# The reciprocal row sums of an attention and soft-MoE kernel: multiplied onto the transposed product through a DMA round trip, with k's factor moved into the maximum's pass and the dispatch logits summed in PSUM

## The chip, the cores and the metric

One core of a Trainium2 chip runs the whole program. The time is the device time of one execution in microseconds (us); three executions of the kernel before gave 566.71, 567.28 and 567.25, median 567.25. Everything is float32, except the last product with the combine weights, which runs in a rounded float32 format.

## The reference, cut to what matters

```python
# attention: 8 batches x 8 heads, 576 tokens, head size 64
scores = q @ k.T / 8
thresh = max(scores, -1) - tau
attn   = exp(where(scores >= thresh, scores, -1e9) - max(scores, -1))
attn   = attn / (sum(attn, -1) + 1e-9)
x      = attn @ v                       # then heads are put side by side: x is 4608 x 512
# soft MoE: 8 experts, 4 slots each (32 slots), phi 512 x 32
logits = x @ phi
d = exp(logits - logits.max(0));  d /= d.sum(0) + 1e-9     # dispatch weights, over all tokens
slot_input = d.T @ x                                       # 32 x 512
slot_out[e] = relu(slot_input[e] @ w1[e]) @ w2[e]          # per expert, 512 -> 1024 -> 512
c = exp(logits - logits.max(1));  c /= c.sum(1) + 1e-9     # combine weights, per token
out = c @ slot_out
```

Two facts matter below. The row sum of the attention weights belongs to a query, so 1 / row sum may be multiplied onto the weights or, later, onto the product with v. And the logits are linear in x.

## The kernel before, in words

**Stages.** The 64 (batch, head) problems are done as 32 pairs of heads, pair p = 4 b + j; after each fourth pair `dispatch(b)` works on the batch. Partitions 0 to 63 hold the first head of the pair, 64 to 127 the second. After the last pair a tail computes the experts (`stage1`, `stage2`) and the combination. The tail's weights w1 and w2 are 64 tiles of 512 KB: 26 are loaded beside the attention (two a pair, from the fourth pair on), the others as SBUF comes free near its end.

**One pair.** 576 queries of two heads are nine tiles i of 128 rows (two heads' last 64 queries share the ninth, `pL`). For each tile: TensorE writes the scores to PSUM (L517, L522). VectorE makes one pass over them (L531), which writes the negated scores to SBUF (`ss`) and their row minimum (`nmx`). GpSimd adds tau to it (`thr`, L547). ScalarE takes the exponential (`p`, L544). VectorE masks by the threshold and sums the row (`r`, L551). TensorE transposes the masked tiles (`ptr`, L441), ScalarE copies them to SBUF (`pTa`, `pTb`, `pTl`), and TensorE multiplies by v (L621, two pieces of 256 and 320 queries). That gives `xT`: 128 rows (two heads' 64 features) by 576 queries. It is transposed once more into `x` (tokens by features).

**Where the row sums and the factor of k go, before.** k is multiplied by 1/8 (`flag8`, 0 where tau is negative) in SBUF by GpSimd before its first use (L497; for the first pair by VectorE, in halves). The reciprocals are made in two pieces: for the ninth tile (L558, L561), which GpSimd then scales itself (`pL`, L565), and for the other eight (L569, L572), which GpSimd multiplies onto `x`, where a query is a partition (L636). As `xT` needs the same factor for the logits, `x` is then transposed back by TensorE (L641) and copied over `xT` by ScalarE (L644). The last pair (`late`) scales its weights instead.

**Dispatch, before.** The four pairs' products with phi stand in four row groups of one PSUM bank (L700), ScalarE copies all 576 columns to SBUF (`l4`), TensorE transposes them (L712), and VectorE adds the four parts (L717, L719). The result is transposed again to get the slots' maximum (L732), the maximum is brought back over the partitions, subtracted (L744, L748) and exponentiated (`d`, `dl`). The tokens 512 to 575 of two batches share tiles, so odd batches do more. `weigh` sums the dispatch weights and the weighted tokens into `csum` and `acc`.

**What sets the order.** Every instruction of the attention is recorded with an engine, an assumed duration, a due time and the buffers it uses. `Order.plan` plays them through: on each engine the ready instruction with the smallest due time is taken, if the buffers it needs are free (`SLOTS` says how many there are; score tiles and other PSUM uses share four regions of two banks). `TABLE` overrides due times one by one. The result is a fixed order on each engine. So an instruction that waits holds up all that stands behind it on its engine, and SyncE's DMAs are issued in the recorded order too.

Of the kernel before, what the change touches and what calls it, by code (L numbers as in the profile page):

```python
# [10 lines left out]
F32 = mybir.dt.float32  # L11
F32R = mybir.dt.float32r
AF = mybir.ActivationFunctionType
# [9 lines left out]
    k=2, q=2, vv=2, r=3, ri=3, nmx=4, thr=4, p2=4, pL=1, pTa=1, pTb=1, pTl=1, l4=1,  # L23
    ss=4, xT=5, x=1, xl=1, ll=1, d=1, M=2, f=2, dl=1,
# [6 lines left out]
AWAY = tuple(range(9))  # L31
# [3 lines left out]
WARM = 38  # L35
FILL = 14
NHOST = 20
TABLE = {}
for _n, _v in (
    ("first", [  # L40
        -69.29, -40.08, -54.39, -166.86, 33.12, -19.81, -19.80, -168.20, -0.40, -236.51, -236.95, -153.88, 373.52, -143.51,
        -213.06, -159.92, -239.98, 369.22, -217.49, None, None, None, None, -253.40, -126.63, -318.67, -88.12, -177.39,
        278.76, -134.26, -253.19, -236.64, -230.43, 370.37, -209.27, None, None, None, None, -339.56, -230.28, -296.07,
        -250.71, 93.46, -214.46, -219.12, 327.41, -239.17, 115.81, -98.67, -235.60, 351.28, -15.35, None, None, None,
        None, 112.02, -216.81, 98.22, -232.40, -233.77, 362.06, -234.27, -288.73, -106.13, -268.80, 322.40, -178.31, 363.65,
        -236.80, None, None, 118.41, -219.40, -224.78, -93.89, -126.64, 366.17, -247.36, 346.23, -178.30, 337.45, -316.13,
        -131.26, -162.52, -225.24, -157.75, 100.52, -243.70, 140.26, -257.76, -282.45, -236.24,
    ]),
    ("pair", [
        371.05, 316.17, 334.99, -1401.66, 316.16, 123.84, 29.03, 245.92, -1430.28, -54.33, 123.33, -50.94, 281.90, -1430.27,  # L50
        -51.83, None, None, None, None, 127.29, 267.41, 123.83, -11.83, 236.94, -1401.65, 331.60, 124.87, 111.68,
        324.56, -1392.66, -17.22, None, None, None, None, 127.78, 273.77, 125.61, 320.90, 124.88, -55.71, 264.20,
        -1401.66, 3.52, 128.01, -29.96, 282.13, -1402.51, -69.32, None, None, None, None, 127.15, 305.89, 128.38,
        -19.31, 318.29, -1392.84, 362.75, 127.50, -39.14, 365.12, -1401.65, -20.82, -1422.29, 119.74, None, None, 135.78,
# [25 lines left out]
    ("soft", [  # L80
        215.59, 346.40, -349.85, 338.95, 233.69, 238.87,
    ]),
    ("new", [
        921.26, -1421.98, 51.86,
    ]),
):
# [1022 lines left out]
```

## Time and profile before

| | us |
|---|---|
| profiled execution, whole | 567.02 |
| its span, first to last instruction | 565.2 |
| PE busy | 536.4 (95%) |
| DVE busy | 476.1 (84%) |
| ACT busy | 458.2 (81%) |
| POOL busy | 257.9 (46%) |
| attention and dispatch, to the last score tiles' end | about 0 to 489 |
| tail | about 489 to 565 |

PE is TensorE, DVE VectorE, ACT ScalarE, POOL GpSimd; SPq is SyncE's queue, which issues all DMAs. A busy PE is not PE at its peak, since matmuls are pipelined and their ends modelled. A row of the timeline gives the start, the duration, the engine, the line and operation, the tiles written and read, how many instructions were merged, and in square brackets the idle time before it with what ended it. A row of the groups gives busy time and mean ns of one after the first bar, idle time before them after the second. A row of the windows gives, for one stretch, the busy time of PE, PEld (weight loads), DVE, ACT and POOL with instruction counts, then the granted clock, the share of the DMA engines in use and GB/s. The mean granted clock of the execution was 0.985.

### The profile page before, as it was taken

What the parts mean: (1) busy time and instruction counts of PE and PEld (TensorE: products, weight loads), DVE (VectorE), ACT (ScalarE), POOL (GpSimd) and SP (SyncE); (2) the same over time, 40 slices, a digit from 0 to 9 for tenths busy, and PEclk for the clock granted to TensorE, in tenths of its full rate; (3) what the DMA queues carried; (4) which work ended last, traced back from release to release, by engine and by line L of the source; (5) the groups of instructions that cost most, each with busy time, mean ns of one, the idle gap of its engine ahead of it and who ended that gap; (6) DMA issues with size and microseconds to landing.
All of it is one profiled execution on the core that took longest, in us unless ns stands there. A gap on an engine that the chain in (4) does not pass through costs nothing. (4 is left out here: it accounts for less than half of the span.)

```text
span 565.2 us, 17532 instructions
## 1 busy us (share of the span) xinstructions
PE 536.4 (95%) x6652; PEld 341.4 (60%) x6652; DVE 476.1 (84%) x1342; ACT 458.2 (81%) x784; POOL 257.9 (46%) x489
## 2 busy tenths in 40 slices
PE   8799999999999999999999999999999998899990
PEld 7566665666566666666666656666666565544470
DVE  5899998999999999998999899999999899322192
ACT  3699998999889999999899989998999889411171
POOL 1555553455345544554455545555555347311030
PEclk9799999999999999999999999999999999999996
DMA  7355555465446544432333333333333312899488
GB/s 170 70 160 164 163 161 154 121 188 177 102 127 178 167 132 140 102 94 52 81 88 89 88 89 87 88 89 87 89 87 88 88 63 54 319 404 409 194 357 313
DMA packets 31988, 82.99 MB, mean 147 GB/s; under 512 B 4640, under 2 KB 12832, under 8 KB 31904
## 3 DMA queue, kind: packets, MB, share of 16 engines
q1 hardware_dynamic: 31904, 81.87, 48.3%
q8 instruction: 53, 0.87, 0.7%
q14 instruction: 31, 0.25, 0.1%
HBM read 72.42 MB, written 9.44 MB: 145 GB/s over the span
## 5 line engine op out<-in xcount | busy, mean ns | idle before, releaser
L531 DVE TENSOR_SCALAR_CACHE_REDUCE ss<-ps 128x576 f32<-128x576 f32 x288 | 209.2, 749 | 23.4 <-ACT l L446 8.1
L547 POOL TENSOR_SCALAR thr<-nmx,pabs 128x1 f32<-128x1 f32 x288 | 130.0, 453 | 177.7 <-DVE ss L531 165.8
L551 DVE SCALAR_TENSOR_TENSOR p<-ss,thr,p 128x576 f32<-128x576 f32 x256 | 205.2, 823 | 3.8 <-POOL thr L547 2.7
L544 ACT ACTIVATE p<-ss,nmx 128x576 f32<-128x576 f32 x256 | 190.4, 781 | 13.0 <-DVE ss L531 13.0
L517 PE MATMUL ps<-k,q 64*128 64x288 f32 x1024 | 165.6, 430 | 3.9 <-POOL k L497 1.8
L441 PEld LDWEIGHTS ps<-ident,p 64*128 64x128 f32 x2304 | 92.9, 140 | 29.5 <-DVE p L551 7.0
L441 PE MATMUL ps<-ident,p 64*128 64x64 f32 x2304 | 105.2, 226 | 3.9 <-DVE ss L531 1.9
L517 PEld LDWEIGHTS ps<-k,q 64*128 64x128 f32 x1024 | 84.9, 190 | 36.1 <-ACT pTb L446 8.8
L446 ACT COPY pTb<-ps 128x1024 f32<-128x1024 f32 (+1 forms) x95 | 83.7, 881 | 2.6 <-PE ps L441 1.4
L621 PE MATMUL ps<-pTb,vv 128*64 128x320 f32 x512 | 76.0, 439 | 2.1 <-ACT pTa L446 1.8
L446 ACT COPY pTa<-ps 128x1024 f32<-128x1024 f32 x64 | 65.7, 1026 | 2.3 <-PE ps L441 2.1
L621 PE MATMUL ps<-pTa,vv 128*64 128x256 f32 x512 | 62.3, 385 | 1.5 <-DVE ss L531 0.8
L621 PEld LDWEIGHTS ps<-pTb,vv 128*64 128x64 f32 x512 | 34.1, 136 | 31.6 <-ACT pTa L446 3.1
L621 PEld LDWEIGHTS ps<-pTa,vv 128*64 128x64 f32 x512 | 33.9, 136 | 27.7 <-DVE ss L531 11.8
L621 PE MATMUL ps<-pTl,vv 128*64 128x256 f32 (+1 forms) x256 | 41.9, 406 | 0.0
L446 ACT COPY xT<-ps 128x256 f32<-128x256 f32 (+1 forms) x63 | 25.2, 400 | 13.5 <-PE ps L621 13.5
L446 ACT COPY pTl<-ps 128x256 f32<-128x256 f32 x64 | 23.8, 372 | 13.1 <-PE ps L441 12.3
L636 POOL TENSOR_TENSOR x<-x,ri 128x512 f32<-128x512 f32 x31 | 33.1, 1069 | 1.6 <-ACT x L446 1.5
L558 POOL TENSOR_SCALAR ri<-r 128x1 f32<-128x1 f32 (+1 forms) x36 | 20.0, 555 | 23.2 <-DVE pL L551 21.4
L565 POOL TENSOR_SCALAR pL<-pL,ri 128x576 f32<-128x576 f32 x32 | 26.5, 830 | 8.4 <-DVE ri L561 5.7
L899 POOL TENSOR_TENSOR c<-lall,crow 128x512 f32<-128x512 f32 x9 | 9.3, 1043 | 39.9 <-PE ct L433 39.9
L497 POOL TENSOR_SCALAR k<-k,flag 128x576 f32<-128x576 f32 x31 | 23.8, 769 | 7.0 <-DMA k<-in_kT 6.4
(134 smaller groups left out, 564.8 us busy)
## 6 DMA issues: line engine op xcount, KB each, us to landing
w<-in_w SPq DMA_DIRECT2D x44, 512.0 KB, 6.6
q<-in_qT SPq DMA_DIRECT2D x62, 288.0 KB, 4.3
vv<-in_vt SPq DMA_DIRECT2D x32, 320.0 KB, 4.0
host<-in_w SPq DMA_DIRECT2D x20, 512.0 KB, 6.4
k<-in_kT SPq DMA_DIRECT2D x62, 144.0 KB, 4.5
out<-w SPq DMA_DIRECT2D x8, 512.0 KB, 3.3
out<-host SPq DMA_DIRECT2D x8, 512.0 KB, 6.1
out<-host SPq DMA_DIRECT2D x4, 256.0 KB, 4.7
```

Source lines behind the costliest of these rows:

```text
L441: nc.tensor.transpose(out=s[:, g, c:c + 64], in_=ins[g], identity=ident[rows[g], rows[g]], tile_position=(64 * g, 0))
L446: G.add("ACT", 51 + 0.833 * n, nom, lambda: nc.scalar.copy(*io()), r, w)
L497: sc = lambda e, kc=kc: lambda: e.tensor_scalar(out=kt.t[:, kc], in0=kt.t[:, kc], scalar1=flag8, **one)
L517: nc.tensor.matmul(s.t[:, g, 0:HS], qt.t[rows[g], h, c * 128:(c + 1) * 128], kt.t[rows[g], h * HS:(h + 1) * HS], start=True, stop=True, ti ...
L531: dve(674, t + OFF['mx'], [s], [ss, nmx], lambda s=s, ss=ss, nmx=nmx: nc.vector.tensor_scalar(out=ss.t.rearrange("p (a k) -> p a k", a=2), ...
L544: G.add("ACT", 668 if away else 630, t + OFF['ex'], lambda sv=sv, nmx=nmx, view=view, away=away: nc.scalar.activation(view().rearrange("p ...
L547: pool(250, t + OFF['th'], lambda nmx=nmx, thr=thr, away=away: nc.gpsimd.tensor_scalar(out=thr.t, in0=nmx.t, scalar1=1.0 if away else -1.0 ...
L551: fn=lambda sv=sv, thr=thr, view=view, i=i, away=away: nc.vector.scalar_tensor_tensor(out=view().rearrange("p (a k) -> p a k", a=2), in0=sv(),
L558: pool(292, t + OFF['ri'], lambda e=e: nc.gpsimd.tensor_scalar(out=ri.t[:, e], in0=r.t[:, e], scalar1=1e-9, scalar2=1.0, op0=ALU.add, op1= ...
L565: pool(725, t + OFF['sc'], lambda k=k, view=view_: nc.gpsimd.tensor_scalar(out=view(), in0=view(), scalar1=ri.t[:, k:k + 1], **one), [ri[c ...
L621: nc.tensor.matmul(lone(w)[h * 64:(h + 1) * 64, 0:n], vv.t[:, v0:v0 + 64], p0, start=(kb == 0), stop=(kb == 4), tile_position=(0, h * 64), ...
L636: G.add("POOL", 1040, u + 6.8, own="new", r=[ri[0]], w=[x[j]], fn=lambda: nc.gpsimd.tensor_tensor(out=wide(), in0=wide(), in1=ri.t[:, 0:8] ...
```

## The change

- k is no longer scaled. The factor, negated (`nflag8`), takes the place of the constant -1 in the maximum's pass. The first pair loses its two VectorE passes as well.
- 1 / row sum is made once a pair for all nine tiles (`ri`, 128 x 9). Except in the last pair, SyncE writes it to DRAM (`rd`), which makes a row of 1152 numbers of it, and reads it back four times broadcast over 64 partitions into `R` (128 x 576): two heads, queries 0 to 511 and the rest. GpSimd multiplies `xT` by `R`, in place. The scaling of `pL`, the multiplication on `x`, the eight transposes back and ScalarE's copy are gone. There is one `R`.
- The dispatch logits of the four pairs are summed by TensorE in PSUM, with the tokens in four column groups: 128 + 64 columns (the last 64 tokens are computed in all four groups). VectorE takes the slots' minimum of the negated logits straight from PSUM; ScalarE's exponential reads PSUM; weights and logits are transposed afterwards. Each batch handles its own last 64 tokens, with a `ones_left` that is zero on the first 64 partitions and an `xl` whose first 64 rows are zero.
- `st4` is filled in the tail by GpSimd. The order's table is new.

```diff
-    k=2, q=2, vv=2, r=3, ri=3, nmx=4, thr=4, p2=4, pL=1, pTa=1, pTb=1, pTl=1, l4=1,
-    ss=4, xT=5, x=1, xl=1, ll=1, d=1, M=2, f=2, dl=1,
+    k=2, q=2, vv=2, r=3, ri=3, R=1, nmx=4, thr=4, p2=4, pL=1, pTa=1, pTb=1, pTl=1, l4=1,
+    ss=4, xT=5, x=1, xl=1, dT=1, d=1, M=2, f=2,
...
-            sc = lambda e, kc=kc: lambda: e.tensor_scalar(out=kt.t[:, kc], in0=kt.t[:, kc], scalar1=flag8, **one)
-            if p == 0:
-                G.add("DVE", 370, t0 - 9 + hs[0], sc(nc.vector), [], [kt[h] for h in hs])
-            else:
-                pool(730, t0 - 9, sc(nc.gpsimd), [], [kt[h] for h in hs])
...
-                    out=ss.t.rearrange("p (a k) -> p a k", a=2), in0=s.t[:, :, 0:HS], scalar1=-1.0, scalar2=3.4028234663852886e38,
+                out=ss.t.rearrange("p (a k) -> p a k", a=2), in0=s.t[:, :, 0:HS], scalar1=nflag8, scalar2=3.4028234663852886e38,
...
-        if not late:
-            xj = lambda: x.t[:, :, j * 128:(j + 1) * 128]
...
-            G.add("POOL", 1040, u + 6.8, own="new", r=[ri[0]], w=[x[j]], fn=lambda: nc.gpsimd.tensor_tensor(
...
-            G.add("PE", 248, u + 7, own="new", r=[x[j]], w=[w], fn=lambda w=w: [
...
-            G.add("ACT", 477, u + 7.3, own="new", r=[w], w=[xT[0], xT[1]], fn=lambda w=w: nc.scalar.copy(
...
+        if not late:
+            rd = rdram[p]
+            rdb, R = Buf(None), Buf("R")
+            rdb.t = True
+
+            def out_r():
+                nc.sync.dma_start(rd.rearrange("(k p) -> p k", p=128), ri.t)
+
+            def in_r():
+                for g in range(2):
+                    nc.sync.dma_start(
+                        R.t[rows[g], 0:SM].rearrange("q (c p) -> q c p", c=4),
+                        rd[0:2 * SM].rearrange("(o c h p) -> o h c p", o=1, c=4, h=2)[:, g].to_broadcast([64, 4, 128]))
+                    nc.sync.dma_start(R.t[rows[g], SM:S], rd[2 * SM + g * SL:2 * SM + (g + 1) * SL].rearrange(
+                        "(o p) -> o p", o=1).to_broadcast([64, SL]))
+            G.add("SP", RW, u + 1, out_r, [ri[4]], [rdb], more=-2000)
+            G.add("SP", RR, u + 2, in_r, [rdb], [R], more=-1500)
+            pool(1170, u + 5, lambda: nc.gpsimd.tensor_tensor(out=xT.t, in0=xT.t, in1=R.t, op=ALU.mult), [R], [xT[0], xT[1]])
...
+        def logits():
+            for o, q in ((slice(0, 128), lambda c: slice(c * 128, c * 128 + 128)), (slice(128, 192), lambda c: slice(SM, S))):
                 for k in range(HP):
+                    for c in range(4):
+                        nc.tensor.matmul(
+                            lone(wl)[c * 32:(c + 1) * 32, o], phi_sb[:, k, :], xT[k].t[:, q(c)], start=(k == 0),
+                            stop=(k == HP - 1), tile_position=(0, 32 * c), skip_group_check=True)
...
+        dve(269, u + 1.3, [wl], [M["own"]] if b else [new["run"]], lambda: nc.vector.tensor_reduce(
+            out=M.t[:, 0:1] if b else new.t[:, 1:2], in_=lone(wl)[:, 0:192], axis=AX.X, op=ALU.max, negate=True))
```

**What the order makes of it**, at the places on which the prediction rests. In the rows a tile's name is followed by the number of its buffer; the operation's line stands first (L5xx and L6xx of the changed file).

TensorE, an ordinary pair, before: the first piece of the product with v, then the transposes of `x` back, then the next tiles.

```order
L621 MATMUL ps_217<-pTa_159,vv_183 64x256 x8
L621 MATMUL ps_217<-pTl_161,vv_183 64x256 x2
L641 MATMUL ps_216<-ident,x_131 128x64 x8
L441 MATMUL ps_218<-ident,p_172 128x64 x16
L522 MATMUL ps_215<-k_176,q_177 64x288 x4
```

And of the change: the second piece of the product with v (L593), then the only transposes of `xT` in a pair (L435), which are those of the pair before.

```order
L593 MATMUL ps_247<-pTb_158,vv_181 64x320 x8
L593 MATMUL ps_247<-pTl_159,vv_181 64x320 x2
L435 MATMUL ps_248<-ident,xT_126 128x64 x8
L435 MATMUL ps_249<-ident,p_167 128x64 x2
L435 MATMUL ps_249<-ident,p_169 128x64 x2
L504 MATMUL ps_250<-k_179,q_180 128x288 x2
L504 MATMUL ps_247<-k_174,q_175 128x288 x2
```

The eight transposes of L641 have no counterpart, and `xT` goes into `x` a whole pair later than it is made.

GpSimd, an ordinary pair of the change: from the reciprocal's first step (`ri`) of one pair to that of the next. Between the thresholds (`thr`) stands one multiplication by `R`, which belongs to the first `ri`.

```order
L539 TENSOR_SCALAR ri_144<-r_141 128x9
L529 TENSOR_SCALAR thr_153<-nmx_151,pabs 128x1
L529 TENSOR_SCALAR thr_154<-nmx_148,pabs 128x1
L529 TENSOR_SCALAR thr_155<-nmx_150,pabs 128x1
L529 TENSOR_SCALAR thr_152<-nmx_149,pabs 128x1
L529 TENSOR_SCALAR thr_153<-nmx_151,pabs 128x1
L529 TENSOR_SCALAR thr_154<-nmx_148,pabs 128x1
L616 TENSOR_TENSOR xT_127<-xT_127,R_147 128x576
L529 TENSOR_SCALAR thr_152<-nmx_149,pabs 128x1
L529 TENSOR_SCALAR thr_155<-nmx_150,pabs 128x1
L529 TENSOR_SCALAR thr_153<-nmx_151,pabs 128x1
L539 TENSOR_SCALAR ri_145<-r_142 128x9
```

VectorE, the same place: it begins with the maximum's pass (L516) whose `nmx_148` feeds the last threshold ahead of the multiplication, and ends with the next pair's reciprocal. Ahead of this piece, from the reciprocal of `ri_144` on, stand three masks (L532) and four such passes.

```order
L516 TENSOR_SCALAR ss_162,nmx_148<-ps_248,nflag_78 128x576
L532 SCALAR_TENSOR_TENSOR p_168,r_142<-ss_160,thr_152,p_168 128x576
L532 SCALAR_TENSOR_TENSOR pL_156,r_142<-ss_163,thr_155,pL_156 128x576
L532 SCALAR_TENSOR_TENSOR p_170,r_143<-ss_161,thr_153,p_170 128x576
L516 TENSOR_SCALAR ss_160,nmx_149<-ps_250,nflag_78 128x576
L516 TENSOR_SCALAR ss_163,nmx_150<-ps_247,nflag_78 128x576
L532 SCALAR_TENSOR_TENSOR p_167,r_142<-ss_162,thr_154,p_167 128x576
L516 TENSOR_SCALAR ss_161,nmx_151<-ps_249,nflag_78 128x576
L532 SCALAR_TENSOR_TENSOR p_167,r_142<-ss_163,thr_155,p_167 128x576
L516 TENSOR_SCALAR ss_162,nmx_148<-ps_250,nflag_78 128x576
L532 SCALAR_TENSOR_TENSOR p_170,r_143<-ss_160,thr_152,p_170 128x576
L542 RECIPROCAL ri_145<-ri_145 128x9
```

The ninth row here is the first mask whose threshold (`thr_155`, from `nmx_150`) stands behind the multiplication on GpSimd.

SyncE, one pair of the fourth to sixteenth, in which weights are loaded too: before, a pair issued q, k, v and two weight tiles. Of the change:

```order
L487 DMA q_180<-in_qT 64x1152 x2
L482 DMA k_179<-in_kT 64x2x288 x2
L415 DMA w_201<-in_w 128x1024
L415 DMA w_202<-in_w 128x1024
L605 DMA rd_221<-ri_145 128x9x1
L609 DMA R_147<-rd_221 64x4x128
L612 DMA R_147<-rd_221 64x64
L609 DMA R_147<-rd_221 64x4x128
L612 DMA R_147<-rd_221 64x64
L489 DMA vv_181<-in_vt 128x640
```

The write of `rd` is issued behind the two weight tiles, and the four reads of `R` wait for it to land; v's load stands behind them.

## The prediction on record

> **What bounds the kernel now.** I read the windows first, then the timeline, then the groups. The multiplication on `x` (L636) comes once a pair and marks the pairs; two marks give an ordinary pair of 13.80 us, and the same mark four pairs apart a batch of 58.56 us.
>
> ```profile
> 301.40 1.04 POOL L636 TENSOR_TENSOR x<-x,ri 128x512 f32<-128x512 f32 x1
> 315.20 1.04 POOL L636 TENSOR_TENSOR x<-x,ri 128x512 f32<-128x512 f32 x1
> ...
> 197.55:256.11 58.56, 57.79 (x770) 37.26 (x768) 55.23 (x159) 54.46 (x94) 29.43 (x58) 1.00 0.45 121
> 301.40:315.20 13.80, 13.65 (x182) 8.92 (x180) 13.25 (x38) 12.92 (x23) 7.59 (x15) 1.00 0.37 90
> ```
>
> The second window says it: PE is busy 13.65 of 13.80, DVE 13.25, ACT 12.92, POOL 7.59. PE bounds, DVE and ACT stand close behind, and each waits a little for the others. So only what leaves PE, or makes it wait less, shortens a pair, and another engine takes over soon: removing POOL's work gives nothing by itself. A batch is four pairs (55.2) and 3.4 us of dispatch.
>
> DVE's own cadence shows how near it is. A maximum's pass takes 0.67 us from its start to the next instruction's, a mask 0.74:
>
> ```profile
> 288.31 0.75 DVE L531 TENSOR_SCALAR_CACHE_REDUCE ss<-ps 128x576 f32<-128x576 f32 x1
> ...
> 288.98 0.81 DVE L551 SCALAR_TENSOR_TENSOR p<-ss,thr,p 128x576 f32<-128x576 f32 x1
> ...
> 289.72 0.75 DVE L531 TENSOR_SCALAR_CACHE_REDUCE ss<-ps 128x576 f32<-128x576 f32 x1
> ```
>
> Nine of each are 12.69 us, and the two reciprocals add about 0.2: 12.9 of 13.80.
>
> **The change part by part.**
>
> *Transposes of x back: off the path.* On PE the eight instructions of L641 take 0.30 us from start to start; eight such without a change of tile shape ahead take 0.25 (L441 on `xT`):
>
> ```profile
> 291.69 0.47 PE L641 MATMUL ps<-ident,x 64*128 64x64 f32 x8
> 291.99 0.66 PE L441 MATMUL ps<-ident,p 64*128 64x64 f32 x16
> ...
> 299.84 0.41 PE L441 MATMUL ps<-ident,xT 64*128 64x64 f32 x8
> 300.09 0.66 PE L441 MATMUL ps<-ident,p 64*128 64x64 f32 x16
> ```
>
> The step back from the product's tile shape (0.05) falls on whatever comes next, so a pair loses 0.25 us: 13.80 becomes 13.55. Behind that, the freed work:
>
> ```profile
> L644 ACT COPY xT<-ps 128x512 f32<-128x512 f32 x31 | 18.2, 586 | 0.4
> L636 POOL TENSOR_TENSOR x<-x,ri 128x512 f32<-128x512 f32 x31 | 33.1, 1069 | 1.6 <-ACT x L446 1.5
> L565 POOL TENSOR_SCALAR pL<-pL,ri 128x576 f32<-128x576 f32 x32 | 26.5, 830 | 8.4 <-DVE ri L561 5.7
> L497 POOL TENSOR_SCALAR k<-k,flag 128x576 f32<-128x576 f32 x31 | 23.8, 769 | 7.0 <-DMA k<-in_kT 6.4
> L558 POOL TENSOR_SCALAR ri<-r 128x1 f32<-128x1 f32 x32 | 18.2, 569 | 22.1 <-DVE pL L551 21.4
> L572 DVE RECIPROCAL ri<-ri 128x8 f32<-128x8 f32 x31 | 6.1, 196 | 0.0
> ```
>
> ACT loses a copy of 0.59 a pair, POOL 1.07 + 0.83 + 0.77 and one step of `ri`, and gains one multiplication of 576 instead of 512 columns, 1.07 x 576 / 512 = 1.20. PE waits in part for ACT's copies; of the 0.15 us it idles in a pair and its waits inside the busy time I count 0.10 as gained, an estimate between 0 and 0.59. Sum: 0.35 a pair, 31 pairs, **-10.9**.
>
> *k's factor in the maximum's pass.* A constant becomes a value per partition. No pass of this kind with such a value is in the trace; the smallest pair of rows that differs in it (on 128x1) has 203 ns with (`nabs`) against 153 without (`pabs`):
>
> ```profile
> L356 DVE TENSOR_SCALAR nabs<-tau_sb 128x1 f32<-128x1 f32 x1 | 0.2, 203 | 0.0
> L358 DVE TENSOR_SCALAR pabs<-nabs 128x1 f32<-128x1 f32 x1 | 0.2, 153 | 0.0
> ```
>
> From 0 to 0.07 a pass (the mask, which reads such a value, is 0.07 longer than the pass). I take 0.05: 0.45 a pair on DVE, less one reciprocal (0.1): 12.9 + 0.35 = 13.25. The cover is DVE's wait for PE, 13.45 - 13.25 = 0.2 a pair, so **0**; without the cover DVE is the bound.
>
> *The round trip of 1 / row sum.* What waits for `R` is POOL's multiplication, behind it the thresholds, and for these DVE's masks. By the rows of the order, from the end of a reciprocal stand five passes and three masks ahead of the multiplication (5.6 us), then four masks and three passes (5.0) until the mask that needs the second threshold behind it. Less the multiplication (1.20), two thresholds at 0.26 (below) and the hops between engines (0.2), `R` may land 8.7 us after the reciprocal, 9.1 with passes 0.05 longer. What it takes, by the nearest DMAs (size, us from issue to landing) and by SyncE's issues in one pair (start, duration):
>
> ```profile
> tau_sb<-in_tau SPq DMA_DIRECT2D x1, 0.5 KB, 2.6
> phi_sb<-in_phi SPq DMA_DIRECT2D x1, 64.0 KB, 2.7
> vv<-in_vt SPq DMA_DIRECT2D x32, 320.0 KB, 4.0
> w<-in_w SPq DMA_DIRECT2D x44, 512.0 KB, 6.6
> q<-in_qT SPq DMA_DIRECT2D x62, 288.0 KB, 4.3
> k<-in_kT SPq DMA_DIRECT2D x62, 144.0 KB, 4.5
> ...
> 245.58 0.26 POOL L547 TENSOR_SCALAR thr<-nmx,pabs 128x1 f32<-128x1 f32 x1
> ...
> 105.84 1.16 SPq L495 DMA_DIRECT2D q<-in_qT  x2
> 107.09 1.29 SPq L490 DMA_DIRECT2D k<-in_kT  x2
> 108.69 0.33 SPq L502 DMA_DIRECT2D vv<-in_vt  x1
> 109.08 0.90 SPq L421 DMA_DIRECT2D w<-in_w  x2
> ```
>
> The write of `rd` is 1152 pieces of 4 bytes. `tau_sb` has 128 such pieces (2.6 us) and `phi_sb` 512 pieces of 128 bytes (2.7), so 384 more pieces cost 0.1: low end 2.7. If all of `phi_sb`'s time went by pieces, 2.7 x 1152 / 512 = 6.1: high end. I take 3.5, nearer to what the two rows' difference says. The reads: issues of 0.65 (as k, 64 rows of two runs) and 0.33 (as v), four in all, so the last starts after 0.65 + 0.33 + 0.65 = 1.6; it lands after 2.7, or 4.0 if like v. With 0.4 for the two waits on semaphores: 0.4 + 3.5 + 1.6 + 2.7 = **8.2 us**, from 7.4 to 12.1. Inside 8.7 to 9.1, so hidden, by half a microsecond.
>
> The Trainium skill, page "DMA: Bandwidth & Descriptors", section "Rules for kernel authors", speaks against this write: a run whose last dimension isn't contiguous becomes one descriptor per element, and one should rearrange. That is the cause of the 1152 pieces; by the rule the landing lies toward the 6.1 us and the sum becomes the first rival below, while the two DMA rows speak for the low end. No row here shows such a store.
>
> In 13 pairs (the fourth to the sixteenth) two weight tiles are issued just ahead of it:
>
> ```profile
> 107.00:114.50 7.50, 7.50 (x94) 4.99 (x92) 7.16 (x23) 6.68 (x14) 5.78 (x10) 1.00 1.00 290
> ```
>
> From 1.2 us after q's first issue the DMA engines are full for 7.5 us (share 1.00, 290 GB/s, 2.2 MB). Now v goes earlier, so q, k and weights (two loads each: 576 + 288 + 1024 KB, 1.9 MB) end 7.7 us after q's first issue. That issue waits for the old k, whose last score tile (the last row of PE's piece) is the sixth row of DVE's piece: 5.6 + 3 x 0.74 + 0.67 = 8.5 us after a reciprocal. The next reciprocal and with it `rd` comes 5 us later, and its data would start 1.2 us behind that, at 6.2. So `rd` waits 1.5 us more: 9.7. Then the loop from reciprocal to reciprocal is 9.7 + 1.2 + 0.7 (thresholds and hops) + 2.3 (two masks, a pass, the reciprocal) = 13.9 instead of 13.45: +0.45 in 13 pairs, **+5.9**.
>
> *Dispatch.* The logits on PE, before, and what DVE and ACT did with them:
>
> ```profile
> 262.36 1.18 PE L700 MATMUL ps<-xT,phi_sb 128*32 128x320 f32 x16
> 263.47 0.46 PE L441 MATMUL ps<-ident,xT 64*128 64x64 f32 x8
> ...
> L717 DVE TENSOR_REDUCE lall<-ps 128x128 f32<-128x512 f32 x8 | 5.5, 692 | 0.2
> L719 DVE TENSOR_REDUCE lall<-ps 64x32 f32<-64x128 f32 x8 | 2.3, 294 | 2.4 <-PE ps L712 2.3
> L744 DVE TENSOR_TENSOR d<-lall,ps 128x128 f32<-128x128 f32 x8 | 2.2, 281 | 0.6 <-PE ps L441 0.6
> L446 ACT COPY l<-ps 128x320 f32<-128x320 f32 x8 | 3.7, 462 | 0.5 <-PE ps L700 0.5
> ```
>
> From start to start PE took 1.11 us for 576 columns in four groups at once. Now each group takes 192 columns from each of four pairs, 768: 1.11 x 768 / 576 = 1.48, +0.37. Sixteen transposes and two more for the maximum become eight and eight: about -0.2. The left tokens' products now come in each batch: +0.1. Together +0.25 on PE in 8 batches, **+2.0**. DVE loses over 1 us a batch (L717, L719, L744 against one minimum over 192 columns and a copy), ACT's work stays about equal; both lie beside PE and count 0.
>
> *Start and end.*
>
> ```profile
> 4.31 0.37 DVE L497 TENSOR_SCALAR k<-k,flag 128x288 f32<-128x288 f32 x1 [0.54 <-DMA k<-in_kT]
> ...
> 490.55 6.87 DMA host<-in_w
> 497.44 10.77 DMA host<-in_w
> ```
>
> The first pass over k goes: at most 0.4, counted 0. In the last dispatch the chain over `l4`, L712 and L717 is shorter, by about 2 us of such instructions and hops; but in the chain of waits the experts' weights are what ends last from 490.55 on, so not all of it shows: **-1**, from 0 to -2. The tail is untouched.
>
> Sum: 567.02 - 10.9 + 5.9 + 2.0 - 1.0 = 563.0. The profiled execution is 0.2 under the median 567.25, within the runs' spread, so I predict **563.0**.
>
> **The rivals.**
>
> *R is late in every pair (slower).* The mechanism is the loop above: POOL stands at the multiplication, the thresholds behind it are late, and DVE's masks with them. It decides where `R` takes more than 13.45 - 4.2 = 9.25 us after the reciprocal; each 0.1 beyond costs 3.1 us over 31 pairs. With `rd` at the high end, 6.1, `R` takes 10.8, in the 13 pairs 12.3: (10.8 - 9.25) x 18 + (12.3 - 9.25) x 13 = 68 on top of 557.1 (the sum without its 5.9): about 625. With 4.5 it takes 9.2 and 10.7: 0 + 1.45 x 13 = 19, about 576. For it: 1152 pieces are more than any DMA of the trace has, and the slack is half a microsecond. Against: two DMAs of 128 and 512 pieces land alike.
>
> *DVE becomes the bound (no change).* At 0.07 a pass and with DVE's present idle of 0.55 a pair kept, a pair is 12.9 + 0.53 + 0.4 = 13.8: nothing is gained, `R` has time, and the sum is 567.0 + 2.0 - 1.0, about 567 to 568. For it: three engines within 7% of each other. Against: PE and ACT, on which DVE waits today, are both relieved.
>
> *The round trip is quick and PE waits less (faster).* `rd` lands in 2.7, `R` in 7.4 and beside the weights in 8.9, all hidden; ACT's copy frees 0.3 a pair instead of 0.1: 567.0 - 0.55 x 31 + 1.0 = about 551.
>
> **How the numbers follow.** Forecast (gain of 3 to 9 us, range of its own 557 to 566): 0.43. Quick round trip (545 to 557): 0.16. DVE the bound (565 to 571): 0.13. R late (568 and up): 0.28, about half of it under 590. Leaving out 0.05 below and 0.13 above, the range is 549 to 592. A difference of 0.2% (1.1 us) is about what a measurement of this kernel can tell from no change. Faster by more: 0.43 + 0.16, less the edge of the forecast, 0.58. Within: 0.09. Slower: 0.28 and a part of DVE's case, 0.33.
>
> **What would show it.** Right: pairs of about 13.45 us in the late part (no weights loading) and 13.9 in the earlier, marked by the multiplication by `R`; PE's busy share as now; ACT about 0.6 a pair lower; the idle time ahead of POOL's multiplication small and ended by ACT's copy of `xT`, or by the DMA of `R` in the 13 pairs alone. R late: POOL idle ahead of it by that DMA in every pair, and DVE waiting for `thr`. DVE the bound: its idle time near 0.2 a pair, the pass over 0.79 long instead of 0.75. Wrong altogether: `rd` landing over 5 us after its issue, or a wait for k or q, whose loads now stand behind the reads of `R`.

## The result, and the profile after

The changed kernel takes 772.94 us (median of 4, 769.21 to 773.64) against 567.20 in the same comparison: a ratio of 1.362, 95% interval 1.357 to 1.366. The forecast was 563.0 with a range up to 592. The profiled execution's span is 771.9 us, its mean granted clock 0.895.

The chain of waits that ended last, by engine, first of the kernel before, then of the change; then the change's chain by line and the groups of the steps in question (busy time and mean ns of one; idle time before it and what ended most of that).

```profile
PE 19%; ACT 9%; DVE 4%; DMA 3%; issue 2%; POOL 2%; SPq 0%; DVEq 0%; ACTq 0%; POOLq 0%
...
DMA 50%; PE 14%; DVE 11%; issue 9%; SPq 8%; POOL 3%; ACT 2%; another core or an unknown queue 1%; POOLq 0%; DVEq 0%; ACTq 0%
DMA rd<-ri 36%; DMA R<-rd 11%; DVE ss L516 5%; SPq L609 5%; PE ps L593 4%; DMA host<-in_w 4%; DVE p L532 3%; SPq L612 3%; PE ps L435 2%; POOL xT L616 2%; PE so L923 2%; POOL thr L529 1%; PE ps L675 1%; PE ps L504 1%; PE h L889 1%
...
L532 DVE SCALAR_TENSOR_TENSOR p<-ss,thr,p 128x576 f32<-128x576 f32 x256 | 204.6, 813 | 124.8 <-POOL thr L529 121.6
L516 DVE TENSOR_SCALAR_CACHE_REDUCE ss<-ps,nflag 128x576 f32<-128x576 f32 x288 | 226.6, 814 | 55.7 <-PE ps L504 20.4
...
L616 POOL TENSOR_TENSOR xT<-xT,R 128x576 f32<-128x576 f32 x31 | 43.9, 1415 | 229.0 <-DMA R<-rd 221.2
```

Before, PE had the largest share of that chain, of which the profile could follow only a part, and transfers 3%; now transfers have half, and the write of `rd` alone is 36% of the span. GpSimd waits 221 us in all for `R` ahead of its multiplication (L616), and the masks of VectorE (L532) wait 122 us for the thresholds behind it. The window of one pair, marked by the multiplication, with PE, PEld, DVE, ACT and POOL busy, the clock, the DMA share and GB/s:

```profile
510.23:530.59 20.36, 13.76 (x158) 8.42 (x158) 13.89 (x37) 11.85 (x20) 5.20 (x11) 0.83 0.34 80
```

A pair takes 20.36 us instead of 13.80 and no engine fills it. The timeline of that pair, rows of GpSimd, VectorE and SyncE's queue, shows the loop:

```profile
510.23 1.40 POOL L616 TENSOR_TENSOR xT<-xT,R 128x576 f32<-128x576 f32 x1 [9.14 <-DMA R<-rd]
...
512.14 0.82 DVE L532 SCALAR_TENSOR_TENSOR p<-ss,thr,p 128x576 f32<-128x576 f32 x1 [5.38 <-POOL thr L529]
...
514.37 0.21 DVE L542 RECIPROCAL ri<-ri 128x9 f32<-128x9 f32 x1
...
514.60 0.38 SPq L605 DMA_DIRECT2D rd<-ri  x1
524.74 0.58 SPq L609 DMA_DIRECT2D R<-rd  x1
...
527.59 0.61 SPq L612 DMA_DIRECT2D R<-rd  x1
...
530.59 1.40 POOL L616 TENSOR_TENSOR xT<-xT,R 128x576 f32<-128x576 f32 x1 [8.17 <-DMA R<-rd]
```

The write is issued 0.02 us after the reciprocal's end (514.58). The first read waits for it until 524.74: **10.1 us** (8.9 to 11.5 over the 31 pairs). The last read is issued 2.85 later and the multiplication starts 3.0 after that: 16.0 from the reciprocal to the multiplication. With the multiplication (1.4), the threshold (0.5) and mask, pass, mask up to the next reciprocal's end (2.4) that is the period. The clock (0.83 in this window) is low too; which part of the time that costs was not tried.

### The profile page after: what moved, and what is told of

Its sections match the earlier page's. It is cut to its first block, busy times and chain, and to the rows that moved or that the text cites. A ratio compares the mean times of both kernels' runs of the same rounds, so it can differ in the third digit from the quotient of the medians.

```text
span 771.9 us, 17739 instructions
## 1 busy us (share of the span) xinstructions
PE 596.8 (77%) x6774; PEld 368.8 (48%) x6774; DVE 483.7 (63%) x1288; ACT 449.1 (58%) x757; POOL 191.3 (25%) x392
## 4 chain that ended last, share of the span: by engine, by line
DMA 50%; PE 14%; DVE 11%; issue 9%; SPq 8%; POOL 3%; ACT 2%; another core or an unknown queue 1%; POOLq 0%; DVEq 0%; ACTq 0%
DMA rd<-ri 36%; DMA R<-rd 11%; DVE ss L516 5%; SPq L609 5%; PE ps L593 4%; DMA host<-in_w 4%; DVE p L532 3%; SPq L612 3%; PE ps L435 2%; POOL xT L616 2%; PE so L923 2%; POOL thr L529 1%; PE ps L675 1%; PE ps L504 1%; PE h L889 1%
## 5 line engine op out<-in xcount | busy, mean ns | idle before, releaser
L532 DVE SCALAR_TENSOR_TENSOR p<-ss,thr,p 128x576 f32<-128x576 f32 x256 | 204.6, 813 | 124.8 <-POOL thr L529 121.6
L516 DVE TENSOR_SCALAR_CACHE_REDUCE ss<-ps,nflag 128x576 f32<-128x576 f32 x288 | 226.6, 814 | 55.7 <-PE ps L504 20.4
L504 PE MATMUL ps<-k,q 64*128 64x288 f32 x1024 | 184.3, 466 | 20.8 <-ACT xT L440 12.7
L435 PE MATMUL ps<-ident,p 64*128 64x64 f32 x2304 | 118.0, 242 | 76.7 <-DVE p L532 55.3
L435 PEld LDWEIGHTS ps<-ident,p 64*128 64x128 f32 x2304 | 103.5, 154 | 111.0 <-issue 69.1
L504 PEld LDWEIGHTS ps<-k,q 64*128 64x128 f32 x1024 | 93.5, 205 | 58.8 <-ACT xT L440 17.0
L616 POOL TENSOR_TENSOR xT<-xT,R 128x576 f32<-128x576 f32 x31 | 43.9, 1415 | 229.0 <-DMA R<-rd 221.2
L593 PE MATMUL ps<-pTb,vv 128*64 128x320 f32 x512 | 78.0, 446 | 2.6 <-ACT pTl L578 2.6
L593 PE MATMUL ps<-pTa,vv 128*64 128x256 f32 x512 | 70.7, 424 | 0.4 <-ACT pTa L440 0.3
L593 PEld LDWEIGHTS ps<-pTb,vv 128*64 128x64 f32 x512 | 34.7, 138 | 39.6 <-DVE ss L516 7.3
L593 PEld LDWEIGHTS ps<-pTa,vv 128*64 128x64 f32 x512 | 37.3, 151 | 21.5 <-issue 6.4
L675 PE MATMUL ps<-xT,phi_sb 128*32 128x64 f32 (+1 forms) x512 | 17.7, 300 | 35.1 <-POOL xT L616 35.1
L593 PE MATMUL ps<-pTl,vv 128*64 128x256 f32 (+1 forms) x256 | 43.2, 413 | 0.0
L675 PEld LDWEIGHTS ps<-xT,phi_sb 128*32 128x32 f32 x512 | 13.8, 139 | 40.1 <-POOL xT L616 37.0
L440 ACT COPY x<-ps 128x512 f32<-128x512 f32 x32 | 18.8, 588 | 18.9 <-PE ps L504 10.1
L509 PE MATMUL ps<-k,q 64*64 64x288 f32 x256 | 29.2, 535 | 0.1
## 6 DMA issues: line engine op xcount, KB each, us to landing
w<-in_w SPq DMA_DIRECT2D x44, 512.0 KB, 10.2
host<-in_w SPq DMA_DIRECT2D x20, 512.0 KB, 10.1
```

Source lines behind the costliest of these rows:

```text
L435: nc.tensor.transpose(out=s[:, g, c:c + 64], in_=ins[g], identity=ident[rows[g], rows[g]], tile_position=(64 * g, 0))
L440: G.add("ACT", 51 + 0.833 * n, nom, lambda: nc.scalar.copy(*io()), r, w)
L504: nc.tensor.matmul(s.t[:, g, 0:HS], qt.t[rows[g], h, c * 128:(c + 1) * 128], kt.t[rows[g], h * HS:(h + 1) * HS], start=True, stop=True, ti ...
L509: nc.tensor.matmul(s.t[rows[a], g, 0:HS], qt.t[rows[g], a, SM:S], kt.t[rows[g], a * HS:(a + 1) * HS], start=True, stop=True, tile_position ...
L516: dve(674, t + OFF['mx'], [s], [ss, nmx], lambda s=s, ss=ss, nmx=nmx: nc.vector.tensor_scalar(out=ss.t.rearrange("p (a k) -> p a k", a=2), ...
L532: fn=lambda sv=sv, thr=thr, view=view, i=i: nc.vector.scalar_tensor_tensor(out=view().rearrange("p (a k) -> p a k", a=2), in0=sv(), scalar ...
```

## The experiments

Each is compared with the kernel before on its own chip (566.3 to 567.3 us).

**1. No round trip.** The write and the four reads are left out.

```diff
-                nc.sync.dma_start(rd.rearrange("(k p) -> p k", p=128), ri.t)
+                pass
...
-                for g in range(2):
+                for g in range(0):
...
+        nc.vector.memset(kinds["R"][0], 1.0)
```

> The changed kernel without the write of rd and the four reads of R: R holds 1 throughout, so the output lacks the division by the row sums; the order on PE, DVE, ACT and POOL is that of the changed kernel. Theory (the exposed round trip is the whole loss, the rest of the change is a small gain): POOL's idle ahead of L616 falls from 229 us to under 10, a pair is about 13.5 us, the time 552 to 564 us. Rival (the rest costs too: the longer maximum's pass, the dispatch, the new order): over 567 us, with DVE busy over 97% of a pair or PE waiting at another place. Rival (the round trip only hides other waits that then appear): 600 us or more.

575.19 us (574.42 to 576.16), ratio 1.015 (1.013 to 1.017). So the round trip costs 197.8 us, and what is left is still slower than before, which is the rival. Windows of this run, a batch and an ordinary pair:

```profile
213.71:274.51 60.80, 58.83 (x788) 38.23 (x788) 55.48 (x154) 53.31 (x91) 26.50 (x44) 0.97 0.37 99
...
241.71:255.16 13.45, 13.45 (x172) 8.84 (x172) 13.45 (x38) 12.64 (x22) 6.81 (x11) 1.00 0.36 94
```

The pair is 13.45 us, as forecast. The batch is not: 60.80 less four pairs leaves 7.0 for dispatch, where it was 3.4. The timeline of that dispatch, rows of PE and VectorE:

```profile
257.60 1.53 PE L675 MATMUL ps<-xT,phi_sb 128*32 128x128 f32 x64
...
261.23 0.60 PE L593 MATMUL ps<-pTl,vv 128*64 128x256 f32 x4
...
261.88 0.36 DVE L680 TENSOR_REDUCE M<-ps 128x1 f32<-128x192 f32 x1 [2.36 <-PE ps L593]
...
262.64 0.34 PE L435 MATMUL ps<-ident,l 64*128 64x64 f32 x4 [0.81 <-ACT l L440]
```

The minimum over the logits (L680) waits not for the logits, whose last product (L675) ends at 259.1, but for the next product with v (L593), which ends at 261.8. That product writes the other half of the PSUM region which the logits were given half of. ScalarE's copies wait for the minimum, and PE, which takes its work in order, waits for the copies.

**2 and 3. The same bytes in fewer pieces.**

```diff
-                nc.sync.dma_start(rd.rearrange("(k p) -> p k", p=128), ri.t)
+                nc.sync.dma_start(rd.rearrange("(a p t) -> p a t", a=3, t=3), ri.t.rearrange("p (a t) -> p a t", a=3))
```

> The write of rd in 384 pieces of 12 bytes instead of 1152 of 4; same bytes, same reads, same order; the values of R are permuted, so the output isn't the reference's. Theory (cost by pieces: 2.6 us at 128 pieces as for tau_sb, 10.1 at 1152, so 7.3 ns a piece): from the write's issue to the first read's issue 4.5 us, R 10.4 us after the reciprocal, which is 1.15 over the 9.25 us that the order allows, so about 595 us (575 to 620) and pairs of about 14.8 us. Rival (a fixed latency from a DRAM write to a read that depends on it, whatever its shape): still about 10 us and 765 to 775 us. Rival (the four reads with their broadcast are what is slow): write quick, but under 100 us gained.

```diff
-                nc.sync.dma_start(rd.rearrange("(k p) -> p k", p=128), ri.t)
+                nc.sync.dma_start(rd.rearrange("(p k) -> p k", k=9), ri.t)
```

> The write of rd in 128 pieces of 36 bytes (each partition's nine values side by side); same bytes, same reads, same order; the values of R are permuted, so the output isn't the reference's. Theory (cost by pieces): write to first read 2.6 us, R about 8.5 us after the reciprocal, inside the 9.25 us allowed, so hidden: within 5 us of the run without the round trip, about 555 to 567 us. Rival (fixed latency): about 10 us and 765 to 775 us. Rival (cost by 4-byte words rather than pieces): also near 10 us and 770 us.

585.43 us (584.52 to 586.61) with 384 pieces, 584.43 (581.38 to 587.51) with 128. The DMA issues of the two runs, one row of each; the last figure is the median from issue to landing:

```profile
rd<-ri SPq DMA_DIRECT2D x31, 4.5 KB, 3.5
```

```profile
rd<-ri SPq DMA_DIRECT2D x31, 4.5 KB, 2.0
```

The reads are unchanged here, and 187.5 and 188.5 us are gone, so neither they nor a fixed latency of write and read are the cause. It is the form of the write. A cost by pieces was still open; the first of the two was expected at 595, and its write landed a microsecond sooner than 7.3 ns a piece gives. The second was expected within 5 us of the first run and is 9.2 above it, so the trip isn't fully hidden yet.

**4. The kernel before with k's factor in the maximum's pass.**

```diff
-        out=flag8, in0=tau_sb, scalar1=0.0, scalar2=0.125, op0=ALU.is_ge, op1=ALU.mult
+        out=flag8, in0=tau_sb, scalar1=0.0, scalar2=-0.125, op0=ALU.is_ge, op1=ALU.mult
...
-            sc = lambda e, kc=kc: lambda: e.tensor_scalar(out=kt.t[:, kc], in0=kt.t[:, kc], scalar1=flag8, **one)
+            sc = lambda e: lambda: None
...
-                    out=ss.t.rearrange("p (a k) -> p a k", a=2), in0=s.t[:, :, 0:HS], scalar1=-1.0, scalar2=3.4028234663852886e38,
+                    out=ss.t.rearrange("p (a k) -> p a k", a=2), in0=s.t[:, :, 0:HS], scalar1=flag8, scalar2=3.4028234663852886e38,
```

> The kernel before with one part of the change alone: k isn't scaled by GpSimd, its negated factor is the per-partition value of the maximum's pass. Theory (the pass is 65 ns longer, 0.59 us a pair on DVE, of which the present DVE idle of 0.55 us hides most): pass mean about 815 ns against 749, DVE busy about 13.8 of a pair of about 13.9, so 567 to 573 us. Rival (the longer pass in the changed kernel comes of its waits or of its clock, not of the per-partition value): pass 749 ns, 565 to 567 us. Rival (relieving POOL of 0.77 us a pair speeds the thresholds): under 565 us.

564.18 us (563.88 to 564.77) against 566.78, ratio 0.995 (0.994 to 0.997). The group of the pass, before and in this run:

```profile
L531 DVE TENSOR_SCALAR_CACHE_REDUCE ss<-ps 128x576 f32<-128x576 f32 x288 | 209.2, 749 | 23.4 <-ACT l L446 8.1
...
L531 DVE TENSOR_SCALAR_CACHE_REDUCE ss<-ps,flag 128x576 f32<-128x576 f32 x288 | 225.9, 808 | 15.1 <-ACT l L446 7.1
```

The value per partition makes the pass 59 ns longer (808 against 749) and the kernel still gains 2.6 us, where 567 to 573 was expected. This version is faster than both kernels. That GpSimd's relief is the gain is argued, not shown.

**5. No round trip, and the logits in a region of their own.** Added to the first run:

```diff
-        wl = bank_of(b == B - 1)
+        wl = Buf("s")
```

> The run without the round trip (575.2 us), but the dispatch logits get a PSUM region of their own instead of half of one whose other half takes the next product with v; the division by the row sums is left out as there. Some tiles change PSUM regions, a few rows of the order swap places. Theory (without the round trip the loss of 8 us against before is the dispatch: the minimum over the logits, L680, waits for the product with v that PE writes into the other half of its region, 16.5 us in 7 batches, and PE then waits in order for the copies behind it): L680's wait for L593 is gone, a batch falls from 60.4 to about 58.4 us, the time to 558 to 566 us. Rival (the wait only changes its name, PE needs those copies at the same place): 573 to 577 us. Rival (a whole region taken away from the score tiles costs more than it gives): over 577 us.

555.29 us (554.76 to 556.15), 19.9 less than the first run, ratio 0.980 (0.977 to 0.983). Windows of a batch and a pair, then the rows of a dispatch on VectorE and PE:

```profile
204.53:261.80 57.27, 57.25 (x788) 37.65 (x788) 55.43 (x154) 53.11 (x91) 26.53 (x45) 1.00 0.40 105
232.54:245.98 13.44, 13.44 (x172) 8.84 (x172) 13.44 (x38) 12.63 (x22) 6.78 (x11) 1.00 0.37 94
```

```profile
250.26 0.35 DVE L680 TENSOR_REDUCE M<-ps 128x1 f32<-128x192 f32 x1
...
252.58 0.34 PE L435 MATMUL ps<-ident,l 64*128 64x64 f32 x4
252.76 0.29 PE L435 MATMUL ps<-ident,dT 64*128 64x64 f32 x4
```

No idle time stands before the rows of this dispatch any more. A dispatch is 57.27 - 4 x 13.44 = 3.5 us. The two halves of a region are two banks, and a region is one PSUM tile of the program. With the logits in a tile of their own the wait is gone, so it came of the shared tile. That the chip itself would not need it is not shown: no run reads one half unguarded while the other is written. The Trainium skill, page "PSUM — Partial Sum Buffer", section "PSUM bank collisions raise a hardware error", asks for a guard by bank and group of partitions, so by it this wait wasn't needed; no run here tries it.

**6. The write by itself.** Eleven DMAs behind the last output of the first run, one at a time.

```diff
+    flat, far = probe[0:1152], probe.rearrange("(k p s) -> p k s", p=128, s=16)
...
+    nc.sync.dma_start(flat.rearrange("(k p) -> p k", p=128), src)
...
+    nc.sync.dma_start(far[:, :, 0], src)
```

> The run without the round trip, with eleven DMAs behind the last output, each issued when the one before has landed, while nothing else runs; the division by the row sums is left out. Theory (a cost per piece of the write, of the DMA itself and not of what runs beside it): 128 pieces of 36 bytes 2.0 us from issue to landing; 1152 pieces of 4 bytes about 10 us, 384 of 12 bytes 3.5, 9 of 512 bytes 2, 576 of 4 bytes about 5.5; 1152 pieces 64 bytes apart, of 4 or 8 bytes, also about 10; reading 1152 pieces of 4 bytes about 10. Rival (neighbouring 4-byte writes by different partitions hinder one another): pieces 64 bytes apart land in under 5 us. Rival (only writes are slow): the read of 1152 pieces lands in under 5 us. Rival (the traffic beside it made it slow): 1152 pieces land in under 5 us here.

SyncE's queue; each row is issued when the DMA of the row ahead has landed, so the difference of two starts is what the earlier one took. Each figure is one DMA of one execution:

```profile
574.26 0.39 SPq L1022 DMA_DIRECT2D probe<-so_sb  x1
585.18 0.37 SPq L1023 DMA_DIRECT2D probe<-so_sb  x1
588.55 0.33 SPq L1024 DMA_DIRECT2D probe<-so_sb  x1
590.03 0.35 SPq L1025 DMA_DIRECT2D probe<-so_sb  x1
591.26 0.60 SPq L1026 DMA_DIRECT2D probe<-so_sb  x1
602.24 0.39 SPq L1027 DMA_DIRECT2D probe<-so_sb  x1
605.38 0.36 SPq L1028 DMA_DIRECT2D probe<-so_sb  x1
608.61 0.36 SPq L1029 DMA_DIRECT2D so_sb<-probe  x1
610.94 0.51 SPq L1030 DMA_DIRECT2D so_sb<-probe  x1
```

| row | what | us |
|---|---|---|
| L1022 | 1152 x 4 bytes, side by side (the change's write) | 10.9 |
| L1023 | 384 x 12 bytes | 3.4 |
| L1024 | 128 x 36 bytes | 1.5 |
| L1025 | 9 x 512 bytes | 1.2 |
| L1026 | 576 x 4 bytes, side by side, from 64 partitions | 11.0 |
| L1027 | 1152 x 4 bytes, 64 bytes apart | 3.1 |
| L1028 | 1152 x 8 bytes, 64 bytes apart | 3.2 |
| L1029 | load of 1152 x 4 bytes | 2.3 |

My theory, a cost per piece, fell: 1152 pieces cost 3.1 us when they lie apart, and half as many side by side cost as much as all. The rival stands: small writes of different partitions to neighbouring addresses are slow, with nothing running beside them. And of the two directions tried only the write is, since the load of 1152 pieces takes 2.3.

**7. The same in the kernel.** As many pieces, as small, 64 bytes apart, in one DRAM region that all pairs share and that is filled at the start.

```diff
-    rdram = [dr.tile([N9 * 128], F32, name=f"rd{p}") for p in range(NP - 1)]
+    rdram = [dr.tile([N9 * 128 * 16], F32, name="rd")] * (NP - 1)
...
-                nc.sync.dma_start(rd.rearrange("(k p) -> p k", p=128), ri.t)
+                nc.sync.dma_start(rd.rearrange("(k p s) -> p k s", p=128, s=16)[:, :, 0], ri.t)
```

> The changed kernel with one edit: the 1152 pieces of 4 bytes are written 64 bytes apart, as many and as small as before; the four reads take the same bytes as before from a region filled with ones at the start, in which only every sixteenth value is a reciprocal, and wait for the write as before, so the output isn't the reference's. Theory now (4-byte writes by different partitions into the same 64 bytes hinder one another): write to first read about 3.3 us as for 384 pieces (3.5), so 580 to 592 us. Rival (the cost is per piece): about 10 us and 765 to 775 us.

587.49 us (584.32 to 588.75): of the 772.94, 185.5 are gone by the distance alone. A write and the first read behind it in SyncE's queue:

```profile
307.10 0.38 SPq L607 DMA_DIRECT2D rd<-ri  x1
310.35 0.59 SPq L611 DMA_DIRECT2D R<-rd  x1
```

3.25 us instead of 10.1. That settles the main cause. Beside the weight loads the same step takes up to 5.6 us in this run.

**8. How near is too near.** The run of single DMAs again, with other distances and numbers.

```diff
+    at = lambda s, n=1: probe[0:1152 * s].rearrange("(k p s) -> p k s", p=128, s=s)[:, :, 0:n]
+    nc.sync.dma_start(at(64)[:, :, 0], src)
...
+    nc.sync.dma_start(at(1)[:, 0:1, 0], src[:, 0:1])
```

> As the run of single DMAs behind the last output, with the distance of the 1152 4-byte pieces at 256, 64, 32, 16, 8 and 4 bytes, then 8-, 16- and 32-byte pieces side by side, then 128, 144 and 288 4-byte pieces side by side. Theory (writes into one 64-byte line go one behind another, about 0.6 us each): 256 and 64 apart 3.1 us, 32 apart about the same, 16 apart (four in a line) 3.5 to 4, 8 apart (eight) about 6, 4 apart (sixteen) 10.9; side by side 8-byte pieces (eight in a line) about 6, 16-byte 3.5, 32-byte 3; 128 and 144 pieces side by side, though few, also 10 to 11 us. Rival (the number of pieces in neighbouring order matters, not the line): 128 pieces side by side under 3 us.

SyncE's queue of this run, read as above:

```profile
576.74 0.37 SPq L1023 DMA_DIRECT2D probe<-so_sb  x1
579.68 0.36 SPq L1024 DMA_DIRECT2D probe<-so_sb  x1
583.14 0.36 SPq L1025 DMA_DIRECT2D probe<-so_sb  x1
586.83 0.36 SPq L1026 DMA_DIRECT2D probe<-so_sb  x1
592.79 0.36 SPq L1027 DMA_DIRECT2D probe<-so_sb  x1
603.47 0.36 SPq L1028 DMA_DIRECT2D probe<-so_sb  x1
608.46 0.36 SPq L1029 DMA_DIRECT2D probe<-so_sb  x1
612.77 0.36 SPq L1030 DMA_DIRECT2D probe<-so_sb  x1
615.01 0.33 SPq L1031 DMA_DIRECT2D probe<-so_sb  x1
622.30 0.33 SPq L1032 DMA_DIRECT2D probe<-so_sb  x1
625.03 0.60 SPq L1033 DMA_DIRECT2D probe<-so_sb  x1
630.36 0.34 SPq L1034 DMA_DIRECT2D probe<-so_sb  x1
```

1152 pieces of 4 bytes take 2.9 us 64 bytes apart (L1023), 3.5 at 32, 3.7 at 16, 6.0 at 8 and 10.7 side by side (L1027); pieces of 8 bytes side by side 5.0 (L1028), of 16 bytes 4.3, of 32 bytes 2.2. So for as many pieces the distance sets the time, as expected. But 128 pieces side by side (L1031) took 7.3, and 144 from 16 partitions in nine rows (L1032) only 2.7, where the theory of one 64-byte line said 10 to 11 for both. That theory is refuted, and in what unit the writes collide stays open.

One count orders these rows, though it was made after the runs and none tests it: the pieces that fall into the same 256 bytes, if the region starts on such a boundary. With 64 of them a write took 10.7 to 11.0 (1152 and 576 pieces; 7.3 where there are only 128 in all), with 32 it took 5.0 to 6.0 (8 bytes apart; 8-byte pieces; the 288 pieces of L1033, which lie 8 bytes apart), with 16 to 21 it took 2.7 to 4.3, with 8 or fewer 1.5 to 3.5. Counted in 512 bytes, the 576 pieces (11.0) would stand with the 1152 that lie 8 bytes apart (6.0), and in 128 bytes the 144 pieces (2.7) with the 288 (5.3).

**9 to 12. Can the change be kept?** Four versions that write 9 rows of 512 bytes. In the first two, PE transposes the reciprocals into a PSUM buffer of their own and ScalarE copies them, both placed by the planner; the logits have their own region.

```diff
+            G.add("PE", 120, u + 1, lambda: nc.tensor.transpose(
+                out=lone(fw)[0:N9, 0:128], in_=ri.t, identity=ident), [ri[4]], [fw], mode=WHOLE, own="fix")
+            G.add("ACT", 160, u + 1.2, lambda: nc.scalar.copy(R.t[0:N9, 0:128], lone(fw)[0:N9, 0:128]), [fw], [R], own="fix")
...
+                nc.sync.dma_start(rd.rearrange("(k p) -> k p", p=128), R.t[0:N9, 0:128])
```

> The changed kernel with the reciprocals transposed by PE (128 x 9 to 9 x 128), copied by ACT into R's buffer and written as 9 pieces of 512 bytes; the reads as before; the logits in a region of their own as in the run before this. Computes all. Theory (pieces are the cost): the write lands in about 2 us, R is late only beside the weights: 5 to 12 us above the run without the round trip that has the same region, so 563 to 578 us. Rival (the round trip itself, four issues and two landings, is too long for this order): 600 us or more. Rival (PE's extra transpose waits for the reciprocal in order and stops the scores): 580 to 600 us with PE waiting for DVE ri.

```diff
-RR = 2000
+RR = 3500
```

> As the run with rows of 512 bytes, but the planner is told 3500 ns instead of 2000 for the reads of R, which moves the multiplication a threshold or two later on POOL. Theory (what is left of the round trip's cost is the multiplication standing too early where weights load): POOL's idle ahead of it by the DMA under 5 us, and 3 to 8 us less than the run with 2000. Rival (the later multiplication makes the transposes of xT late, or the new order is worse by itself): same or slower than with 2000.

581.38 us (581.07 to 582.54) and 581.79 (580.84 to 582.37): 26 above the fifth run. The group of the multiplication in the second of them:

```profile
L620 POOL TENSOR_TENSOR xT<-xT,R 128x576 f32<-128x576 f32 x31 | 45.9, 1479 | 7.7 <-ACT xT L440 7.7
```

It no longer waits for `R` at all, and nothing is gained by that. The planner made another order around the two new operations; which part of it costs the 26 us was not separated. The next version keeps the order of the fifth run and puts the transposes into the unused columns of the next score tile:

```diff
+                            for e in range(2):
+                                nc.tensor.transpose(out=s.t[0:N9, e, HS:HS + 64], in_=carry[-1][2].t[rows[e]],
+                                                    identity=ident[rows[e], rows[e]], tile_position=(64 * e, 0))
...
+            nc.scalar.copy(to.t[0:N9, 0:128].rearrange("k (e q) -> k e q", e=2), s.t[0:N9, :, HS:HS + 64])
```

> A version meant to keep the change and lose both faults. The order and the logits' own PSUM region are those of the run of 555.3 us; the reciprocals of a pair are transposed by PE (two 64 x 9 pieces) into the unused columns of the next score tile's region, copied by ACT into R's buffer, and written as 9 rows of 512 bytes; the four reads follow at once. Computes all. Theory: the write lands in 1.3 to 2 us, R is there 8.6 to 10.1 us after the reciprocal, about when xT is; PE has about 0.15 us a pair more: 557 to 567 us. Rival (R still arrives behind xT, above all beside the weights): 567 to 585 us with POOL waiting for R. Rival (PE's transposes wait for the reciprocal in order and hold the scores): 575 us or more with PE waiting for DVE ri.

566.30 us (564.45 to 567.11), ratio 0.999 (0.997 to 1.000): no difference from before, at the far end of what was expected. Two rows of its waits (total, times, longest):

```profile
POOL xT L646 <- DMA R<-rd: 17.5, 13, 3.0
DVE ss L552 <- ACT R L470: 16.8, 23, 1.6
```

`R` is late in 13 pairs, which is the rival's wait; but nine of these come after the last weight load was issued (213.6 us), and the rival had most of them beside the weights. The second row was new: VectorE's pass waits for ScalarE's copy; both read the same tile. The last version records the copy behind the pass:

```diff
-        if eng == "ACT" and carry and t >= carry[0][0] + SOON:
+        if eng == "DVE" and carry and carry[0][1] in passed:
```

> As the run with the transposes in the score tile's region (566.3 us), but ScalarE's copy of the reciprocals is recorded behind VectorE's pass over that tile instead of ahead of it. Computes all. Theory (what kept that run from its 557 to 567 is that the pass waited for the copy, 16.8 us in 23 pairs, since the readers of one PSUM tile go in recorded order): this wait is gone, ScalarE waits a little for VectorE instead, R is 0.5 us later: 556 to 562 us, faster than both kernels. Rival (R, later still, holds POOL and with it the thresholds): 564 to 572 us with DVE waiting for thr. Rival (the transposes' cost on PE is what counts): 564 to 568 us with PE as busy as before.

589.27 us (585.97 to 589.92), a miss. The wait of the pass is gone. In its place `R` is late more often, masks wait for exponentials, and PE's weight loads (PEld) for the copy; which of these makes the 23 us over the run before was not separated:

```profile
POOL xT L645 <- DMA R<-rd: 25.1, 19, 2.8
...
DVE p L567 <- ACT p L561: 19.5, 24, 1.2
...
ACT R L469 <- issue: 17.5, 28, 0.9
PEld ps L437 <- ACT R L469: 15.4, 25, 1.1
```

## Why the prediction was wrong, point by point

The runs split the 205.7 us (each row the difference of two medians; they add up to 206.2, since the kernel before took 566.7 on the chip of run 5 and 567.2 beside the change):

| part | runs | us |
|---|---|---|
| pieces side by side instead of 64 bytes apart | change against 7 | +185.5 |
| the rest of the round trip | 7 against 1 | +12.3 |
| the minimum's wait in dispatch (the shared region) | 1 against 5 | +19.9 |
| all else | 5 against before | -11.5 |

- **The step that failed: "The write of `rd` ... I take 3.5", with 2.7 and 6.1 as its ends.** It took 10.1, where the prediction itself named over 5 us as the sign of being wrong altogether. Both rows that priced it, `tau_sb` and `phi_sb`, are loads; run 6 has a load of 1152 pieces at 2.3 us, near the low end, and the write at 10.9. I let loads bound a write, so no end of the range could hold it. The number of pieces, over which I argued, was not the price.
- The other terms of the trip held: the last read's issue to the multiplication was 3.0 against 2.7 (2.7 in the pair before, 507.50 to 510.23), the issues 1.9 to 2.9 against 1.6.
- **The rival "R is late in every pair" was the right mechanism**, with its threshold: 557.1 + (16.0 - 9.25) x 31 = 766, against 772.9 measured. That it comes so close is partly luck: the sum has no wait in dispatch, and takes one pair's 16.0 for all. Its price, 576 to 625, carried the same error, so its chance of 0.28 didn't help the range.
- The weights' contention was put at +5.9. With a quick write the trip costs 9.2 (run 3), 10.2 (run 2) and 12.3 (run 7). In run 3 it is of the forecast's kind: GpSimd's seven waits for `R` (17.0 us) all lie between 48 and 200 us, while weights load, and later there is none. The write then takes 3.5 to 4.9 us to the first read in ten of the 13 pairs, and 1.4 to 2.4 in the pairs without weights: about 2.5 us more, where 1.5 was forecast.
- **Dispatch, "+2.0 ... both lie beside PE and count 0", missed a wait.** Without it a dispatch is 3.5 us against 3.4, so the arithmetic on PE held; with it 7.0. The order showed it: L675 and the first piece of L593 behind it write the two halves of one PSUM region, and L680, which reads the first half, is recorded behind both.
- Transposes and copies gone: 13.45 a pair forecast, 13.44 measured. That doesn't show that PE's saving set the pair. VectorE was to be busy 13.25, with 0.2 to spare; in run 5 it is busy 13.44 of 13.44, since the pass grew by 59 to 65 ns, not 50. Two engines now fill the pair, which of them sets it wasn't separated, and the match to 0.01 is in part luck. A further gain on PE alone would probably bring little.
- The rival "DVE becomes the bound" keeps an idle of 0.55 in its words but adds 0.4 in its sum; with 0.55 a pair would be 13.98. The pair of run 5 shown above leaves VectorE no idle time at all.
- k's factor alone was counted 0; it brings 2.6 us (run 4).
- The sum without its 5.9 was 557.1; run 5, without the trip and without the wait in dispatch, has 555.3.
- The Trainium skill's rule on strided last dimensions (page "DMA: Bandwidth & Descriptors", section "Rules for kernel authors"), cited in the prediction, pointed the right way. One descriptor per element, of which it speaks, is not what cost here: run 7 has as many pieces and 3.25 us. The same page, section "Specifications", says that transfers under 512 bytes do a read-modify-write. That fits colliding writes, yet the pieces of 36 bytes and those 64 bytes apart are under 512 bytes too and landed in 1.5 to 3.1, so by itself it doesn't tell them from the slow ones.

## What to carry to other kernels

Price a write by a row of a write, and where the trace has none, let the range say so. Before you count a saving on one engine, look what the next engine needs in the same stretch. A column of small values that partitions write side by side to DRAM is worth a transpose first: 9 rows of 512 bytes landed in 1.2 us where 1152 words took 10.9. Here the best order for that transpose brought the kernel to 566.3 us, level with before, so where it goes in the order has a price too. When two results share a PSUM tile, look up in the order who writes its other half before counting a reader as free.

## What the hardware showed that was not expected

- 1152 4-byte writes to DRAM from 128 partitions: 10.7 to 10.9 us side by side, 6.0 at 8 bytes' distance, 2.9 to 3.1 at 64, with nothing else running. Other traffic isn't needed for the slow form: in the kernel it took 8.9 to 11.5. A quick write does feel it: 128 pieces of 36 bytes took 1.4 to 2.4 us to the first read, and up to 4.9 beside the weights (run 3).
- Half as many such pieces took the same 11.0 us, and 128 of them 7.3.
- GpSimd's multiplication took 1.4 us while VectorE mostly waited (the change: mean 1415 ns) but 1.9 in the ordinary pairs of run 1, where VectorE is busy throughout. The forecast had 1.2.
